# Fused sigmoid attention, Fourier mixing with an MLP and a gated convolution on one core: another way to turn float64 weights into float32, and one more feed-forward group by seven products

## Chip, cores, metric

One core of one Trainium2 chip runs the whole program. Its engines are TensorE (PE; weight loads are PEld), VectorE (DVE), ScalarE (ACT), GpSimd (POOL) and SyncE (SP, which issues the transfers). The metric is device time in microseconds (us), the median of several executions. The reports below come from one further execution, taken by the hardware profiler.

## What is computed

```python
def reference(q, k, v, moe, moe2):                 # q, k, v: 4 x 12 x 448 x 64, float32
    a = sigmoid(q @ k.T / sqrt(64) - log(448)) @ v          # per batch and head
    x = a.transpose(0, 2, 1, 3).reshape(4, 448, 768)
    u = x + real(fft(fft(x, axis=1), axis=2))
    un = (u - mean(u)) / sqrt(var(u) + 1e-6)                # over the last axis
    x = u + maximum(un @ w_ch1, 0) @ w_ch2                  # 768 -> 3072 -> 768
    gate = sigmoid(causal_conv(x, conv_w))                  # 5 taps along the sequence
    return (gate * (x @ w_val)) @ w_out                     # 768 -> 768 -> 768
```

The four weight matrices arrive as float64, drawn from a normal distribution.

## The kernel before

Everything is written by one planner. Jobs are Python generators that yield "my next instruction belongs to this engine and needs these tiles"; the planner (class `Board`, with the estimated durations of class `Clock`) keeps an estimated time per engine and places the waiting jobs' instructions by rank and time, so the order on every engine is fixed when the kernel is built. All instructions are recorded at the helper line L219, so the rows below are told apart by their tiles. An engine runs its list in order: what stands behind a waiting instruction waits too.

The stages, by time in the profiled execution:

- 0 to 182 us: attention. A step is 8 matmuls `ps_s<-q,k`, one ACT sigmoid `sg<-ps_s` and 8 matmuls `ps_m<-sg,v`; there are 84 steps. The Fourier transform (`cd`, `cs`, `k,e`) of each batch, its row means (`ones,tt`) and its variance's factor (`tt,ones`) are placed in between. The first weight blocks are converted here.
- 182 to 800 us: the feed-forward part, in NG = 6 groups of 512 hidden columns. `up` of a group is done in one of two forms. The regular form (`up`, for the groups below REG) does the four batches one by one: 288 matmuls of 128x448 per group, with hi and lo halves of float16 (hi x hi, hi x lo, lo x hi). The form with seven products (`quad`, for the other groups) takes batches in pairs and, by sums of halves of activations (`tb`) and of weights (`w1hi`, `w1lo`), does 4 quads of 63 matmuls, 252 per group, and joins the results on DVE (`c`, `w1lo`, `h`), ACT (`c`, `h`) and POOL (`h<-c,h`). `down` is the same for all groups: 288 matmuls `ps_m<-h,w`, added by DVE into `acc`.
- The sums `tb` are made on POOL by `sums`: a first half once batch 3 is normalised, a second half per pair once `up` of the last regular group has passed that pair.
- 800 us to the end: gates, values (`xs,wv`) and output (`gh,wo`) of the four batches.

Weights: `convert` (L447) fetches a float64 piece of 128x384 (tile `w`), and makes a float32 out of its two 32-bit halves. ACT takes the absolute value of the upper half (`wabs<-w`), DVE clamps it and takes the maximum of each row in the same instruction (`wabs,mx<-wabs`, with a read of the accumulator behind it), DVE shifts (`wabs<-wabs`, or `wf<-wabs` for the first blocks), and two DVE instructions with two inputs bring in the low bits and the sign (`wabs<-w,wabs`). The float32 pieces are spilled to DRAM and read back for scaling and splitting. `peak` (L411) turns a block's row maxima into one maximum: DVE puts them on a diagonal (`pd`), PE multiplies it by ones, DVE reduces and works out the scale (`factors`). PE executes 24 such matmuls in the program. There are 120 pieces: 8 for each block of w_ch1 or w_ch2 (w1[g], w2[g]; 16 per group), and 12 each for w_val and w_out. The blocks w1[0], w2[0] and w1[1], the first 24 pieces, go straight into `wf` without a spill; the others are spilled. A fetched tile has three buffers, and the next fetch of SP waits until the piece that held the buffer is done.

Of the kernel before, what the change touches and what calls it, by code (L numbers as in the profile page):

```python
# [59 lines left out]
DRAM = bass.MemoryType.DRAM  # L60
FIRST = 7
TABLE = 8
ABS_BY = "ACT", "DVE"
W_RANK = 3.5
LEAST = 2.0 ** (896 // 8 - 127)


class Clock:
# [91 lines left out]
    def note(self, e, op, a, k):  # L160
        if op == "matmul":
            out, w, x = a
            n = x.free_size()
            full = x.partition_size() > 64 or w.free_size() > 64
            passes = 1 if x.dtype != F32 else 4 if full else 1
            cost = passes * (max(n / 2400, 0.045) + (0.0018 if passes == 1 else 0.006))
            mode = full, out.partition_size() > 64 or not full
            if mode != self.mode:
                cost += 0.2
                self.mode = mode  # L170
            return self.put("PE", cost, (w, x), (out,), 0.12, tag="mm")
# [170 lines left out]
def body(tc, qd, kd, vd, w1d, w2d, cwd, wvd, wod, cdd, k12d, csd, eyed, out):  # L342
# [68 lines left out]
    def peak(m, nm):  # L411
        yield on("DVE", m, eye)
        t = col(nm + "t")
        V.tensor_reduce(out=t, in_=m, axis=AX.X, op=ALU.max)
        d = keep.tile([128, 128], F32R, tag="pd", bufs=2, name="pd")
        V.tensor_scalar(out=d, in0=eye, scalar1=t, scalar2=None, op0=ALU.mult)
        yield on("PE", d, go=banks(1))
        p = ps_m()
# [4 lines left out]
        done_m(p)
        return g

    def pow2(g, nm, upper=False, e=None):

        e = col(nm + "e") if e is None else e
        if upper:
            V.tensor_scalar(out=e.bitcast(I32), in0=g.bitcast(I32), scalar1=0x07F00000, scalar2=3, op0=ALU.bitwise_and, op1=ALU.logical_shift_left)  # L430
            V.scalar_tensor_tensor(out=e.bitcast(I32), in0=g.bitcast(I32), scalar=0x40000000, in1=e.bitcast(I32), op0=ALU.bitwise_and, op1=ALU.bitwise_or)
        else:
            V.tensor_scalar(out=e.bitcast(I32), in0=g.bitcast(I32), scalar1=0x7F800000, scalar2=None, op0=ALU.bitwise_and)
# [10 lines left out]

    W1N = NT * FG

    def convert(rank, src, m, dst=None, to=None, step=COLS, done=None, hold=None):  # L447

        num = len(src)
        got, ready, gone = [], [], [0] if done is None else done  # L450

        def fetch():
            for k in range(num):
                yield on("SP", go=lambda: gone[0] > k - 3)
                w = ws.tile([128, step], I64, tag="w64", bufs=3, name="w64")
# [17 lines left out]
        board.add(rank, absolute())  # L473
        for k in range(num):
            yield when(lambda: len(ready) > k and (hold is None or hold(k)))
            z, wa = got[k], ready[k]
            lo, hi, f = z[:, :, 0], z[:, :, 1], wa if dst is None else dst[k]
            yield on("DVE", wa)
            if m is None:
                V.tensor_scalar(out=wa, in0=wa, scalar1=LEAST, scalar2=None, op0=ALU.max)  # L480
            else:
                V.tensor_scalar(out=wa, in0=wa, scalar1=LEAST, scalar2=None, op0=ALU.max, op1=ALU.max, accum_out=m[k])
            yield on("DVE", wa)
            V.tensor_scalar(out=f.bitcast(I32), in0=wa.bitcast(I32), scalar1=0x07FFFFFF, scalar2=3, op0=ALU.bitwise_and, op1=ALU.logical_shift_left)
            yield on("DVE", z)
            V.scalar_tensor_tensor(out=f.bitcast(I32), in0=lo, scalar=29, in1=f.bitcast(I32), op0=ALU.logical_shift_right, op1=ALU.bitwise_or)
            yield on("DVE", z)
            V.scalar_tensor_tensor(out=f.bitcast(I32), in0=hi, scalar=-0x40000000, in1=f.bitcast(I32), op0=ALU.bitwise_and, op1=ALU.bitwise_or)
# [1107 lines left out]
```

## Time and profile before

| | |
|---|---|
| median of 3 executions | 1026.77 us (1026.36 to 1028.44) |
| the profiled execution | 1025.13 us |
| its span, first to last instruction | 1023.3 us |
| PE, DVE, ACT, POOL busy | 98%, 77%, 46%, 28% |
| matmuls | 6048 |
| mean granted TensorE clock | 0.996 |

The page gives for every engine the busy time over the span. Matmuls are pipelined and their ends are modelled, so a busy PE is read together with the count of matmuls per stretch. "idle before <-releaser" is time in which an engine stood still ahead of an instruction, and what ended it.

### The profile page before, as it was taken

How to read it: one execution, taken by the hardware profiler on the slowest of the kernel's cores; microseconds unless marked ns; L12 is line 12 of the kernel's file. 1: busy time of each engine (PE TensorE's matmuls, PEld its weight loads, DVE VectorE, ACT ScalarE, POOL GpSimd, SP SyncE). 2: the span in 40 equal slices, each digit the busy share in tenths (PEclk: the TensorE clock that was granted, in tenths of full speed). 3: DMA queues.
4: the chain of work that ended last, by engine and by line, in shares of the span. 5: the costliest groups of instructions: out<-in, count | busy, mean ns of one | idle time of the engine just before them, and what ended most of it. 6: DMA issues, size and time to landing. Idle time of an engine off the chain costs nothing.

```text
span 1023.3 us, 15801 instructions
## 1 busy us (share of the span) xinstructions
PE 1006.0 (98%) x6048; PEld 524.2 (51%) x6048; DVE 791.1 (77%) x1480; ACT 471.4 (46%) x666; POOL 285.8 (28%) x209
## 2 busy tenths in 40 slices
PE   9899899999999999999999999999999999999998
PEld 4344454675555555555555555545555555555554
DVE  4776788888998778968979998989894487767630
ACT  6786767235341354143515451445144687344321
POOL 0103323232768520035503320332033573000000
PEclk9999999999999999999999999999999999999999
DMA  7653240001222366545345435643450120000001
GB/s 232 220 184 99 82 134 11 15 16 47 67 82 70 116 200 224 160 157 187 107 155 183 134 117 176 196 126 114 155 157 30 47 93 1 10 37 37 37 30 70
DMA packets 54547, 110.30 MB, mean 108 GB/s; under 512 B 6456, under 2 KB 30408, under 8 KB 54472
## 3 DMA queue, kind: packets, MB, share of 16 engines
q1 hardware_dynamic: 54472, 109.30, 33.5%
q8 instruction: 47, 0.77, 0.3%
q14 instruction: 28, 0.23, 0.1%
HBM read 84.76 MB, written 24.38 MB: 107 GB/s over the span
## 4 chain that ended last, share of the span: by engine, by line
PE 86%; DVE 8%; issue 2%; ACT 2%; DMA 1%; SPq 0%; DVEq 0%; ACTq 0%
PE ps_m L219 62%; PE ps_s L219 25%; DVE wabs L219 2%; DVE wf L219 1%; DVE tt L219 1%; DVE c L219 1%; DVE acc L219 1%; DVE pm L219 0%; DMA v<-vd 0%; DMA q<-qd 0%; ACT sg L219 0%; ACT h L219 0%; SPq L219 0%; ACT c L219 0%; DVE pd L219 0%
## 5 line engine op out<-in xcount | busy, mean ns | idle before, releaser
L219 PE MATMUL ps_m<-h,w 128*128 128x448 f16 x1728 | 328.8, 353 | 0.0
L219 PEld LDWEIGHTS <-w 128*128 128x128 f16 x2016 | 196.8, 98 | 183.4 <-issue 2.9
L219 PE MATMUL ps_s<-un,w1hi 128*128 128x448 f16 x528 | 143.0, 353 | 0.0
L219 ACT ACTIVATE wabs<-w 128x384 f32<-128x384 f32 x120 | 65.2, 551 | 168.1 <-DMA w<-w2d 44.9
L219 DVE SCALAR_TENSOR_TENSOR wabs<-w,wabs 128x384 int32<-128x384 int32 x192 | 135.9, 708 | 4.7
L219 PEld LDWEIGHTS <-w1hi 128*128 128x128 f16 x888 | 86.3, 98 | 80.0
L219 DVE SCALAR_TENSOR_TENSOR acc<-ps_m,rg,acc 128x448 f32<-128x448 f32 x144 | 97.9, 680 | 35.8 <-PE ps_m L219 32.3
L219 POOL TENSOR_TENSOR w<-wf,w 128x768 f16<-128x768 f32 x24 | 41.1, 1724 | 213.2 <-ACT w L219 213.0
L219 ACT ACTIVATE sg<-ps_s,logb 128x896 f32<-128x896 f32 x84 | 83.9, 1007 | 30.7 <-PE ps_s L219 29.7
L219 PE MATMUL ps_s<-un,w1lo 128*128 128x448 f16 x264 | 93.0, 352 | 0.0
L219 PE MATMUL ps_m<-sg,v 64*64 64x448 f32 x672 | 82.8, 550 | 3.1 <-DVE acc L219 2.1
L219 PE MATMUL ps_s<-q,k 64*64 64x448 f32 x672 | 80.9, 538 | 4.4 <-ACT sg L219 4.4
L219 PE MATMUL ps_m<-xs,wv 128*128 128x448 f16 x432 | 84.6, 353 | 0.0
L219 PE MATMUL ps_m<-gh,wo 128*128 128x448 f16 x288 | 80.8, 352 | 0.0
L219 DVE SCALAR_TENSOR_TENSOR gp<-acc,cw,gp 128x448 f32<-128x448 f32 x84 | 60.3, 718 | 21.9 <-ACT gp L219 19.9
L219 POOL TENSOR_TENSOR h<-c,h 128x896 f16<-128x896 f32 x24 | 46.4, 1934 | 90.2 <-ACT h L219 69.4
L219 DVE TENSOR_SCALAR_CACHE_REDUCE wabs<-wabs 128x384 f32<-128x384 f32 x120 | 65.3, 544 | 2.2 <-ACT wabs L219 2.1
L219 PEld LDWEIGHTS <-w1lo 128*128 128x128 f16 x444 | 43.4, 98 | 40.6
L219 PEld LDWEIGHTS <-wo 128*128 128x128 f16 x432 | 42.3, 98 | 39.5
L219 PEld LDWEIGHTS <-wv 128*128 128x128 f16 x432 | 42.1, 98 | 39.1
L219 ACT ACTIVATE h<-ps_s 128x896 f16<-128x896 f32 x24 | 22.0, 916 | 79.5 <-PE ps_s L219 79.3
L219 PE MATMUL ps_s<-un,w 128*128 128x448 f16 x288 | 57.9, 360 | 0.0
(172 smaller groups left out, 1446.7 us busy)
## 6 DMA issues: line engine op xcount, KB each, us to landing
w<-w1d SPq DMA_DIRECT2D x48, 384.0 KB
w<-w2d SPq DMA_DIRECT2D x48, 384.0 KB
w<-wabs SPq DMA_DIRECT2D x72, 192.0 KB
wf<-w SPq DMA_DIRECT2D x36, 384.0 KB
q<-qd SPq DMA_DIRECT2D x24, 224.0 KB
out<-o SPq DMA_DIRECT2D x24, 224.0 KB
k<-kd SPq DMA_DIRECT2D x23, 224.0 KB
w<-wvd SPq DMA_DIRECT2D x12, 384.0 KB
```

The source lines that it names most:

```text
L219: return f(*a, **k)
```

## The change

1. REG goes from 3 to 2: group 2 is done with seven products too. The second half of `sums` starts when `up` of group 1, not 2, has passed a pair.
2. `convert` works in place in the fetched tile. ACT (or, for the first 24 pieces, ACT or DVE, whichever the planner finds free) makes two passes: the upper half times 2^-112 as float32, and the top byte of the lower half as an integer of three bits. DVE joins the two with two instructions of two inputs. The piece is spilled, and then its magnitudes are summed along the rows by an ACT pass with an accumulator (`w,mx<-f`); for w_val, and where DVE is chosen, DVE takes the exact row maximum with a reduction. The scale exponents are set anew for sums in place of maxima.
3. In `peak`, the matmul with `pd` may be placed on PE only 2.5 us after DVE's estimated time, from PE's 200th us on.
4. `Clock` gives every single-pass matmul 0.0029 instead of 0.0018 us on top of its columns.
5. `pow2` loses the two-instruction form for float64 exponents.

```diff
-UN_EXP = 4
+UN_EXP = -2
...
-REG = 3
+REG = 2
-NABS = 3
+PD = 2.5
...
-ABS_BY = "ACT", "DVE"
+EARLY_BY = "ACT", "DVE"
+LATE_BY = "ACT"
+WBUF = 3
+FBUF = 3
...
-            cost = passes * (max(n / 2400, 0.045) + (0.0018 if passes == 1 else 0.006))
+            cost = passes * (max(n / 2400, 0.045) + (0.0029 if passes == 1 else 0.006))
...
-        yield on("PE", d, go=banks(1))
+        late = ck.at["DVE"] + (PD if ck.at["PE"] > 200 else 0.0)
+        yield on("PE", d, go=lambda: banks(1)() and board.by(late))
...
-                yield when(lambda: len(got) > k and gone[0] > k - NABS)
-                wa = ws.tile([128, step], F32, tag="wabs", bufs=NABS, name="wabs")
-                e = yield on(by, got[k], cost=0.55)
+                yield when(lambda: len(got) > k)
+                w = got[k].bitcast(F32).rearrange("p (n t) -> p n t", t=2)
+                e = yield on(by, w[:, :, 1], cost=0.55)
                 if e == "ACT":
-                    A.activation(out=wa, in_=got[k][:, :, 1].bitcast(F32), func=AF.Abs)
+                    A.activation(out=w[:, :, 1], in_=w[:, :, 1], func=AF.Copy, scale=2.0 ** -112)
                 else:
-                    V.tensor_scalar(out=wa.bitcast(I32), in0=got[k][:, :, 1], scalar1=0x7FFFFFFF, scalar2=None, op0=ALU.bitwise_and)
-                ready.append(wa)
+                    V.tensor_scalar(out=w[:, :, 1], in0=w[:, :, 1], scalar1=2.0 ** -112, scalar2=None, op0=ALU.mult)
+                lo = w.bitcast(I32)[:, :, 0]
+                e = yield on(by, w[:, :, 0], cost=0.55)
+                if e == "ACT":
+                    top = got[k].bitcast(U8).rearrange("p (n t) -> p n t", t=8)[:, :, 3]
+                    A.activation(out=lo, in_=top, func=AF.Copy, scale=2.0 ** -5, bias=-0.484375)
+                else:
+                    V.tensor_scalar(out=lo, in0=lo, scalar1=29, scalar2=None, op0=ALU.logical_shift_right)
+                ready.append(w.bitcast(I32))
+        def join():
...
+                yield when(lambda: len(ready) > k and gone[0] > k - FBUF and (hold is None or hold(k)))
+                lo, hi = ready[k][:, :, 0], ready[k][:, :, 1]
...
+                yield on("DVE", hi, lo)
+                V.scalar_tensor_tensor(out=lo, in0=hi, scalar=-0x80000000, in1=lo, op0=ALU.bitwise_and, op1=ALU.bitwise_or)
+                yield on("DVE", lo, f)
+                V.scalar_tensor_tensor(out=f.bitcast(I32), in0=hi, scalar=3, in1=lo, op0=ALU.logical_shift_left, op1=ALU.bitwise_or)
...
-                V.tensor_scalar(out=wa, in0=wa, scalar1=LEAST, scalar2=None, op0=ALU.max, op1=ALU.max, accum_out=m[k])
-            yield on("DVE", wa)
-            V.tensor_scalar(out=f.bitcast(I32), in0=wa.bitcast(I32), scalar1=0x07FFFFFF, scalar2=3, op0=ALU.bitwise_and, op1=ALU.logical_shift_left)
...
+            if m is not None:
+                e = yield on("DVE" if exact(k) else by, f, cost=0.75)
+                if e == "ACT":
+                    A.activation(out=ready[k].bitcast(F32)[:, :, 1], in_=f, func=AF.Abs, accum_out=m[k])
+                else:
+                    V.tensor_reduce(out=m[k], in_=f, axis=AX.X, op=ALU.max, apply_absolute_value=True)
             gone[0] += 1
```

The program as a whole has 36 matmuls of 128x448 fewer, since one group's `up` goes from 288 to 252. On ACT, 119 passes `wabs<-w` give way to 224 passes `w<-w` and 89 with an accumulator; on DVE, 120 clamps with an accumulator and 120 shifts are gone, 240 joins remain, and 31 reductions and 16 passes come in.

**ACT, in the quads of a late group.** `w_...` are fetched float64 pieces, `f_...` their float32. Before:

```order
L219 ACTIVATE w1lo<-ps_m 128x448
L219 ACTIVATE c<-c 128x896
L219 ACTIVATE h<-c 128x896
L219 ACTIVATE wabs<-w_6310 128x384
L219 ACTIVATE wabs<-w_6345 128x384
L219 ACTIVATE c<-c 128x896
L219 ACTIVATE h<-c 128x896
L219 ACTIVATE w1lo<-ps_m 128x448
L219 ACTIVATE wabs<-w_6386 128x384
L219 ACTIVATE wabs<-w_6452 128x384
L219 ACTIVATE c<-c 128x896
L219 ACTIVATE h<-c 128x896
```

After, in a like place:

```order
L222 ACTIVATE c<-c 128x896
L222 ACTIVATE h<-c 128x896
L222 ACTIVATE w_6520<-w_6520 128x384 x2
L222 ACTIVATE w_6438,mx<-f_6538 128x384
L222 ACTIVATE c<-c 128x896
L222 ACTIVATE h<-c 128x896
L222 ACTIVATE w_6550<-w_6550 128x384 x2
L222 ACTIVATE w1lo<-ps_m 128x448
L222 ACTIVATE w_6520,mx<-f_6568 128x384
L222 ACTIVATE w_6581<-w_6581 128x384 x2
L222 ACTIVATE w_6550,mx<-f_6610 128x384
L222 ACTIVATE c<-c 128x896
```

A piece now has three instructions on ACT, and the last of them, with `mx`, stands behind the first two of the next piece.

**DVE, around the first maximum of w_val** (`wvt` is the row maxima's maximum, `pd` the diagonal, `wvg` the reduction of PE's product). Before:

```order
L219 SCALAR_TENSOR_TENSOR wabs<-w_6386,wabs 128x384
L219 TENSOR_TENSOR c<-ps_s,w1lo 128x896
L219 TENSOR_TENSOR c<-ps_s,c 128x448
L219 SCALAR_TENSOR_TENSOR wabs<-w_6386,wabs 128x384
L219 TENSOR_REDUCE wvt<-mx 128x1
L219 TENSOR_SCALAR pd<-eye,wvt 128x128
L219 TENSOR_SCALAR wabs,mx<-wabs 128x384
L219 TENSOR_SCALAR wabs<-wabs 128x384
L219 SCALAR_TENSOR_TENSOR wabs<-w_6452,wabs 128x384
L219 TENSOR_TENSOR c<-ps_s,c 128x896
L219 SCALAR_TENSOR_TENSOR wabs<-w_6452,wabs 128x384
L219 TENSOR_REDUCE wvg<-ps_m 128x1
```

After:

```order
L222 SCALAR_TENSOR_TENSOR acc_104<-ps_m,rg,acc_104 128x448
L222 SCALAR_TENSOR_TENSOR w_6156<-w_6156 128x384
L222 SCALAR_TENSOR_TENSOR f_6208<-w_6156 128x384
L222 TENSOR_REDUCE mx<-f_6208 128x1
L222 TENSOR_REDUCE wvt<-mx 128x1
L222 TENSOR_SCALAR pd<-eye,wvt 128x128
L222 TENSOR_TENSOR c<-ps_m,w1lo 128x448
L222 SCALAR_TENSOR_TENSOR w_6188<-w_6188 128x384
L222 TENSOR_TENSOR w1lo<-ps_m,w1lo 128x448
L222 SCALAR_TENSOR_TENSOR f_6254<-w_6188 128x384
L222 TENSOR_REDUCE wvg<-ps_m 128x1
L222 TENSOR_SCALAR factors<-wvg 128x1
```

A piece has two joins and a reduction where it had four instructions; between `pd` and `wvg` four instructions stand where there were five.

**PE, at the row sums of squares of the last batch** (`ones,tt`) and at the matmuls that spread its factor (`tt,ones`). Before, the sums:

```order
L219 LDWEIGHTS w_770
L219 MATMUL ps_s<-un,w_770 128x448
L219 MATMUL ps_m<-ones,tt 112x1 x24
L219 LDWEIGHTS w_770
L219 MATMUL ps_s<-un,w_770 128x448
```

and the factor, 30 matmuls later:

```order
L219 LDWEIGHTS w_770
L219 MATMUL ps_s<-un,w_770 128x448
L219 MATMUL ps_m<-tt,ones 128x112 x4
L219 LDWEIGHTS w_770
L219 MATMUL ps_s<-un,w_770 128x448
```

After, the second and larger part of the sums (a first part of x8 stands 6 matmuls ahead of it):

```order
L222 LDWEIGHTS w_788
L222 MATMUL ps_s<-un,w_788 128x448
L222 MATMUL ps_m<-ones,tt 112x1 x16
L222 LDWEIGHTS w_788
L222 MATMUL ps_s<-un,w_788 128x448
```

and the factor, 18 matmuls `un,w` and 6 `h,w` later:

```order
L222 LDWEIGHTS w_2431
L222 MATMUL ps_m<-h,w_2431 128x448
L222 MATMUL ps_m<-tt,ones 128x112 x4
L222 LDWEIGHTS w_2431
L222 MATMUL ps_m<-h,w_2431 128x448
```

The sums are split, and the first matmuls `h,w` of `down` of group 0 have moved ahead of the factor; before, they came 102 matmuls behind it. At the first `h,w`, PE has 216 matmuls `un,w` behind it; at the factor of before it had 186.

## Rows read from the trace of the kernel before

**Rows 1.** The page's first part, PE's share: busy us, share, instructions.

```profile
PE 1006.0 (98%) x6048; PEld 524.2 (51%) x6048; DVE 791.1 (77%) x1480; ACT 471.4 (46%) x666; POOL 285.8 (28%) x209
```

**Rows 2.** Chain that ended last: start us, us, what.

```profile
252.16 19.31 PE ps_s L219 x102
...
381.45 54.68 PE ps_m L219 x290
```

**Rows 3.** Stretches of 20 us: busy us and count by engine, PE clock, DMA.

```profile
500.00:520.00 20.00, 20.00 (x108) 10.36 (x106) 19.86 (x27) 4.87 (x7) 9.31 (x6) 1.00 0.04 15
...
680.00:700.00 20.00, 18.74 (x100) 9.59 (x99) 19.04 (x41) 8.71 (x12) 4.72 (x3) 1.00 0.49 147
```

**Rows 4.** PE in order of time: matmuls of `pd` after 200 us that waited.

```profile
293.63 0.33 PE L219 MATMUL ps_m<-pd,ones_r 128*128 128x128 f32 x1 [0.61 <-DVE pd L219]
...
489.85 0.33 PE L219 MATMUL ps_m<-pd,ones_r 128*128 128x128 f32 x1 [0.30 <-DVE pd L219]
...
655.70 0.33 PE L219 MATMUL ps_m<-pd,ones_r 128*128 128x128 f32 x1 [0.44 <-DVE pd L219]
...
686.25 0.30 PE L219 MATMUL ps_m<-pd,ones_r 128*128 128x128 f32 x1 [1.26 <-DVE pd L219]
...
855.96 0.33 PE L219 MATMUL ps_m<-pd,ones_r 128*128 128x128 f32 x1 [0.48 <-DVE pd L219]
```

**Rows 5.** PE in order of time, the three longest waits of attention.

```profile
34.98 0.33 PE L219 MATMUL ps_m<-pd,ones_r 128*128 128x128 f32 x1 [1.19 <-DVE pd L219]
...
47.96 0.98 PE L219 MATMUL ps_s<-q,k 64*64 64x448 f32 x8 [2.72 <-ACT sg L219]
...
178.00 3.72 PE L219 MATMUL ps_m<-sg,v 64*64 64x448 f32 x24 [2.10 <-DVE acc L219]
```

**Rows 6.** PE in order of time, around the last batch's row sums.

```profile
238.41 4.79 PE L219 MATMUL ps_m<-ones,tt 128*112 128x1 f32 x48
...
251.02 1.15 PE L219 MATMUL ps_m<-tt,ones 112*128 112x112 f32 x8 [0.45 <-DVE tt L219]
```

**Rows 7.** Stretches of 2 us behind these sums, columns as in rows 3.

```profile
244.00:246.00 2.00, 2.00 (x7) 0.87 (x6) 1.49 (x1) 1.97 (x3) 2.00 (x2) 0.50 0.03 8
246.00:248.00 2.00, 2.00 (x9) 0.84 (x8) 2.00 (x1) 1.85 (x3) 2.00 (x3) 0.66 0.00 0
```

**Rows 8.** POOL in order of time: the four low halves of w2[0].

```profile
244.45 6.44 POOL L219 TENSOR_TENSOR w<-wf,w 128x768 f16<-128x768 f32 x4
```

**Rows 9.** Groups by form, conversion: busy us, mean ns, idle before.

```profile
L219 DVE TENSOR_SCALAR_CACHE_REDUCE wabs<-wabs 128x384 f32<-128x384 f32 x120 | 65.3, 544 | 2.2 <-ACT wabs L219 2.1
...
L219 ACT ACTIVATE wabs<-w 128x384 f32<-128x384 f32 x119 | 65.0, 553 | 168.1 <-DMA w<-w2d 44.9 <-DMA w<-w1d 35.9 <-DMA w<-wod 29.1
...
L219 DVE TENSOR_SCALAR wabs<-wabs 128x384 int32<-128x384 int32 x96 | 47.3, 493 | 2.7
...
L219 ACT ACTIVATION_READ_ACCUMULATOR xs<-acc 128x1 f32 x8 | 1.5, 187 | 0.0
```

**Rows 10.** Longer stretches, columns as in rows 3: attention; one late group.

```profile
0.00:180.00 180.00, 169.74 (x1580) 81.86 (x1584) 135.51 (x278) 128.50 (x163) 40.87 (x38) 1.00 0.43 138
...
551.00:652.00 101.00, 100.99 (x535) 52.25 (x534) 94.72 (x179) 42.18 (x60) 20.70 (x12) 1.00 0.49 155
```

**Rows 11.** DVE and POOL in order of time, end of attention.

```profile
174.25 1.99 DVE L219 TENSOR_SCALAR wf<-wabs 128x384 int32<-128x384 int32 x1
...
174.12 1.90 POOL L219 TENSOR_TENSOR un<-tt,un 128x896 f16<-128x896 f32 x1 [6.30 <-ACT un L219]
```

**Rows 12.** POOL in order of time: second half of `tb`, first pair.

```profile
443.85 2.04 POOL L219 TENSOR_TENSOR tmp<-un 128x448 f32<-128x448 f16 x2
...
478.56 1.04 POOL L219 TENSOR_TENSOR un<-tmp,un 128x448 f16<-128x448 f32 x1 [1.95 <-ACT un L219]
```

**Rows 13.** Groups by form, joining of the quads, as in rows 9.

```profile
L219 ACT ACTIVATE c<-c 128x896 f32<-128x896 f32 x24 | 22.8, 950 | 59.9 <-DVE c L219 59.9
...
L219 DVE TENSOR_TENSOR c<-ps_s,w1lo 128x896 f32<-128x896 f32 x12 | 13.0, 1087 | 6.9 <-PE ps_s L219 6.9
```

More of the change, by code (lines that the diff above doesn't have):

```diff
@@ L13 @@
 I64 = mybir.dt.int64
+U8 = mybir.dt.uint8
 AF = mybir.ActivationFunctionType
@@ L32 @@
 X_EXP = 3
-W1_EXP = 1
-W2_EXP = 9
-UN_EXP = 4
+W1_EXP = 7
+W2_EXP = 14
+UN_EXP = -2
 X2_EXP = 14
 WV_EXP = 1
-WO_EXP = 9
+WO_EXP = 14
 G_EXP = -10
@@ L424, in peak, with pow2 @@
         return g
-    def pow2(g, nm, upper=False, e=None):
+    def pow2(g, nm, e=None):
         e = col(nm + "e") if e is None else e
[L429 to L433, printed above, removed]
+        V.tensor_scalar(out=e.bitcast(I32), in0=g.bitcast(I32), scalar1=0x7F800000, scalar2=None, op0=ALU.bitwise_and)
         V.tensor_scalar(out=e, in0=e, scalar1=2.0 ** -90, scalar2=2.0 ** 90, op0=ALU.max, op1=ALU.min)
@@ L445, in body, with convert @@
     W1N = NT * FG
-    def convert(rank, src, m, dst=None, to=None, step=COLS, done=None, hold=None):
+    def convert(rank, src, m, dst=None, to=None, step=COLS, done=None, hold=None, exact=lambda k: False):
         num = len(src)
@@ L453, in fetch @@
             for k in range(num):
-                yield on("SP", go=lambda: gone[0] > k - 3)
-                w = ws.tile([128, step], I64, tag="w64", bufs=3, name="w64")
+                yield on("SP", go=lambda: gone[0] > k - WBUF)
+                w = ws.tile([128, step], I64, tag="w64", bufs=WBUF, name="w64")
                 Q.dma_start(out=w, in_=src[k])
-                got.append(w.bitcast(I32).rearrange("p (n t) -> p n t", t=2))
-        by = ABS_BY if rank < 4 else "ACT"
-        def absolute():
+                got.append(w)
@@ L462, in absolute, with parts @@
+        by = EARLY_BY if rank < 4 else LATE_BY
+        def parts():
             for k in range(num):
[L463 to L465 removed]
+                yield when(lambda: len(got) > k)
+                w = got[k].bitcast(F32).rearrange("p (n t) -> p n t", t=2)
+                e = yield on(by, w[:, :, 1], cost=0.55)
                 if e == "ACT":
[L467 removed]
+                    A.activation(out=w[:, :, 1], in_=w[:, :, 1], func=AF.Copy, scale=2.0 ** -112)
@@ new lines, in parts @@
+                ready.append(w.bitcast(I32))
+        def join():
+            for k in range(num):
+                yield when(lambda: len(ready) > k and gone[0] > k - FBUF and (hold is None or hold(k)))
+                lo, hi = ready[k][:, :, 0], ready[k][:, :, 1]
+                f = ws.tile([128, step], F32, tag="f32", bufs=FBUF, name="f32") if dst is None else dst[k]
+                yield on("DVE", hi, lo)
+                V.scalar_tensor_tensor(out=lo, in0=hi, scalar=-0x80000000, in1=lo, op0=ALU.bitwise_and, op1=ALU.bitwise_or)
+                yield on("DVE", lo, f)
+                V.scalar_tensor_tensor(out=f.bitcast(I32), in0=hi, scalar=3, in1=lo, op0=ALU.logical_shift_left, op1=ALU.bitwise_or)
+                joined.append(f)
@@ L472, in convert @@
+        joined = []
         board.add(rank, fetch())
-        board.add(rank, absolute())
+        board.add(rank, parts())
+        board.add(rank, join())
         for k in range(num):
-            yield when(lambda: len(ready) > k and (hold is None or hold(k)))
-            z, wa = got[k], ready[k]
-            lo, hi, f = z[:, :, 0], z[:, :, 1], wa if dst is None else dst[k]
-            yield on("DVE", wa)
-            if m is None:
-                V.tensor_scalar(out=wa, in0=wa, scalar1=LEAST, scalar2=None, op0=ALU.max)
-            else:
-                V.tensor_scalar(out=wa, in0=wa, scalar1=LEAST, scalar2=None, op0=ALU.max, op1=ALU.max, accum_out=m[k])
-            yield on("DVE", wa)
-            V.tensor_scalar(out=f.bitcast(I32), in0=wa.bitcast(I32), scalar1=0x07FFFFFF, scalar2=3, op0=ALU.bitwise_and, op1=ALU.logical_shift_left)
[L485 to L488, printed above, removed]
@@ L489, in convert @@
+            yield when(lambda: len(joined) > k)
+            f = joined[k]
             if to is not None:
@@ L545, in stream @@
         board.add(4, scaling())
-        yield from convert(4, src, ms, None, to, done=done, hold=lambda k: all(e[2] in kept for e in ends[:max(0, sum(x[0] <= k for x in ends) - 1)]))
+        yield from convert(4, src, ms, None, to, done=done, exact=lambda k: next(e[2][0] for e in ends if k < e[0]) == "wv", hold=lambda k: all(e[2] in kept for e in ends[:max(0, sum(x[0] <= k for x in ends) - 1)]))
     def again(key):
```

3 lines of the change are left out of this document (1 added, 2 removed).

## The prediction

> **What bounds the kernel now.** The first view is the page's share of busy time: PE is busy for 98% of the span [rows 1]. Since matmuls are pipelined, that share alone says little, so the second view is the chain that ended last, where long pieces are PE alone: 102 matmuls in 19.31 us and 290 in 54.68 us, 0.189 us each [rows 2]. The third is PE's count in stretches of 20 us: a full one holds 108 matmuls of 128x448, 0.185 us each, even where DVE is busy for 19.86 of 20 us; one with a wait holds 100 [rows 3]. So behind attention the end is set by PE's number of matmuls plus the places where PE stands still, and whatever the other engines gain is worth something only at such a place.
>
> These places are, read from PE in order of time: five matmuls of `pd` after 200 us that waited for DVE, 0.61 + 0.30 + 0.44 + 1.26 + 0.48 = 3.1 us [rows 4]; some waits in attention, the three longest 1.19, 2.72 and 2.10 us [rows 5]; the matmul of the last batch's factor, 0.45 us [rows 6]; and a fall of the clock right behind 48 one-column matmuls that took 4.79 us [rows 6]. The granted clock is 0.50 in the next stretch of 2 us, which is the lower level of 1.2 GHz, and 0.66 in the one behind it [rows 7]. In these 4 us PE made 16 matmuls where 108 per 20 us are 21.6, so the fall cost about 5.6 x 0.189 = 1.1 us at least, and with its edges some 1.7 us (half of the 2 + 0.68/0.5 = 3.4 us at 0.50).
>
> **The matmuls of group 2.** 288 regular ones become 252, at 0.189 us each [rows 2]: 36 x 0.189 = **-6.8 us**. All of them lie on PE in a stretch where nothing else sets the end [rows 3]. The Trainium skill ("Perfetto Trace Analysis", section "Identifying the Most-Contended Engine") says that matmul busy time doesn't show how close TensorE is to its limit, and asks for the weight loads' busy share instead. That share is 51% here [rows 1]; by this rule PE might have room left and the 36 matmuls be worth nothing, and the sum would be 6.8 us less. The counts per stretch [rows 3] speak against it, and I take them.
>
> **The matmuls with `pd` placed later.** Each waits for a short DVE chain that the planner had estimated too early. With 2.5 us of room against waits of 0.30 to 1.26 us [rows 4], all five should be gone: -3.1 us, and I take **-3.0 us**; the bounds are 0, where DVE is late by more than that, and -3.1. What waits behind is the scale on DVE and then the scaling of a block on ACT and POOL, up to 2.5 us later; weight blocks are needed tens of us later, except for w2[0], below.
>
> **The last batch's variance.** The one-column matmuls are split in two runs, x8 and x16 where x24 stood, and `down` of group 0 stands in front of the factor's matmul. The wait of 0.45 us is covered by it, and the fall of the clock, which came after one unbroken run, should be less or gone: 0 to -2.2 us, I take **-2.0 us**. The price of the cover: PE now needs w2[0] at its first `h,w`. POOL finished its low halves at 244.45 + 6.44 = 250.9 us [rows 8]. PE's first `h,w` stands behind 216 matmuls `un,w` where the factor, at 251.0 us, stood behind 186: 251.0 + 30 x 0.189 = 256.7 us, less the 2.2 us above and what attention gains, so 253 to 255 us. The slack is 2 to 4 us; a wait here would take back up to 3 us, with nothing behind it on PE to fill in.
>
> **The conversion.** DVE loses 120 clamps of 0.544 us with their accumulator reads and 120 shifts of about 0.49 us [rows 9], and gets 47 instructions of the same size: some 65 + 59 - 26 = 98 us less, and it waits for ACT's passes instead. ACT loses 119 passes of 0.553 us and gets 224 of them and 89 with an accumulator. No row shows a pass over every eighth byte or one that writes in place; the nearest is the pass over every second word, 0.553 us, and I take that (bounds 0.5 and 1.1 us, twice it). For the accumulating ones I add the 0.187 us of the read [rows 9]: 0.74 us. ACT's net is 105 x 0.553 + 89 x 0.74 = +124 us. A late group has 16 pieces: ACT goes from 42.18 us in a stretch of 101 us to 42.2 + 16 x (0.553 + 0.74) = 63 us, DVE from 94.72 to about 94.7 - 16 x 1.1 = 77 us [rows 10]. Both stay below PE, so behind 200 us this edit is worth **0 us** by itself; PE's 108 per 20 us covers it. If ACT's `c`, `h` come late because a pass ahead of them waits for a transfer or a join, up to +5 us come out.
>
> In attention it is another matter, since PE waits there for `sg` of ACT and `acc` of DVE [rows 5], and ACT is busy for 128.5 of 180 us [rows 10]. By the order, ACT has there 17 passes and 3 accumulations where 13 absolute values stood, +4 x 0.553 + 3 x 0.74 = +4.4 us, and three 128x896 instructions `un` go behind the stage: about the same load, in another order. The wait of 2.10 us came after a shift on DVE that took 1.99 us [rows 11] instead of about 0.49 [rows 9], beside a POOL instruction of 1.90 us that began 0.13 us earlier [rows 11]. Shifts of that kind are mostly gone. The Trainium skill ("SBUF", section "Who interferes with whom") has it that `tensor_scalar` and GpSimd lock each other out of a shared port pair for a whole instruction; the trace agrees with 1.99 us. The same section says that a DVE instruction with two SBUF inputs contends with GpSimd's reads as well, and the joins are such. By the first rule alone the stage would gain 2.1 us, by both it would keep part. I take **-1 us** for the stage: the three waits of rows 5 sum to 6.0 us, any may go and others come. The bounds are -6 and, with ACT's passes at 1.1 us, 17 x 0.55 = +9.
>
> **Group 2 by seven products.** DVE gets five joins per quad of at most 1.087 us, ACT two instructions `c` and two `h` of about 0.95 us [rows 13]: at most 22 and 15 us in a group, from which the regular form's eight `h` on each engine go. Against 77 and 63 us of about 102 this fits. The sums `tb`: the first pair's second half took from 443.85 to 479.6 us on POOL [rows 12], 36 us. It now starts when group 1's `up` passes the pair, about 354 us (half of that `up`'s 288 x 0.189 = 54 us ahead of 381.45 [rows 2]) and, for the second pair, 381 us, so it ends at about 390 and 417 us; the quads of group 2 start when `down` 1 ends, 381.45 + 54.68 = 436 us [rows 2], less what was gained, and the second pair's 24 us later. Slack 40 us: **0 us**.
>
> **The sum.** -6.8 - 3.0 - 2.0 - 1.0 = -12.8 us. The profiled execution was 1025.13 us with a span of 1023.3; the median is 1026.77, 1.6 us above it. 1025.1 - 12.8 = 1012.3, and in terms of the median **1014.0 us**.
>
> **The rivals.**
> *Only the columns, or only the waits.* The waits for DVE turn up at other matmuls of `pd`, or at w2[0], and the 6.8 us remain: about 1026.8 - 6.8 = 1020 us. The rule on weight loads is the same case from the other side: the 36 matmuls give nothing and the waits go, 1026.8 - 6.0 = 1020.8 us. For it: all waits are DVE's, by an estimate of the planner that may be off elsewhere. Against: DVE gets lighter by some 98 us.
> *Attention gets smooth.* The waits of rows 5 go, 6 us in place of 1: 1009 us, or less with smaller ones. For it: DVE's slow shifts go. Against: one of the three waits is ACT's, which gets no lighter there.
> *A piece's round trip (slower).* A fetched tile is now held through two ACT passes, two joins, and the ACT pass with `mx`, which stands behind the next piece's passes and behind `c` and `h`. With three buffers and 16 pieces per 102 us, a round trip of 3 x 102/16 = 19 us is the point from which PE waits for weights. Each us beyond is 16/3 = 5.3 us per group, over four groups 21 us; one us over gives 1014 + 21 = 1035 us. For it: ACT waited 44.9 us for transfers of w2 alone already [rows 9]. Against: it had 168 us idle there, and PE lost nothing.
> *Attention worse.* ACT's passes at twice the price: +9 in place of -1 in the stage, 1014 + 10 = 1024 us, and a little more where the same passes hold up `c` and `h` later: about 1025 to 1028 us, within 0.2%.
>
> **Chances.** Forecast (1010 to 1018 us) 0.60; smooth attention (1004 to 1010) 0.12; only columns or only waits (1018 to 1023) 0.13; attention worse (1025 to 1028) 0.06; round trip 0.09. A measurement of this kernel can tell a difference of about 0.2%, 2 us, from none: faster than 1024.7 us 0.85, within 0.06, slower 0.09. A range of 1006 to 1024 us leaves out the last two and the lower part of smooth attention, under 0.2.
>
> **What would show it.** 6012 matmuls, and full stretches of 108 per 20 us from 260 to 800 us. No `pd` matmul after 200 us with an idle time for DVE. The granted clock near 1.0 between 240 and 250 us, and no wait for w2[0] at the first `h,w`. ACT's passes near 0.55 us, the accumulations near 0.74, ACT at about 59% and DVE near 68%. The forecast is wrong if PE's stretches hold fewer than 108 while ACT is behind with `c` or `sg`, if `tb` or a weight block ends a wait of PE, or if attention ends later than 182 us by more than a few us.

## The result, and the profile after

| | before | after |
|---|---|---|
| median | 1027.43 us (1026.36 to 1028.44, 4 runs) | 1012.05 us (1009.61 to 1014.13, 4 runs) |
| profiled execution, its span | 1025.13, 1023.3 us | 1009.61, 1007.8 us |
| ratio, 95% interval | | 0.985 (0.9824 to 0.9875) |

The change makes the kernel 15.4 us faster; 12.8 had been forecast, in another composition, as the experiments show. The page's first part, to be read against [rows 1]:

```profile
PE 996.7 (99%) x6012; PEld 520.1 (52%) x6012; DVE 701.6 (70%) x1172; ACT 573.1 (57%) x965; POOL 293.3 (29%) x212
```

36 matmuls are gone, DVE lost 90 us and ACT gained 102. Two stretches of 20 us that answer to [rows 3], then attention's and a late group's, which answer to [rows 10] (columns as in [rows 3]):

```profile
500.00:520.00 20.00, 20.00 (x109) 10.38 (x106) 14.08 (x27) 5.73 (x13) 0.00 (x0) 1.00 0.52 168
680.00:700.00 20.00, 20.00 (x109) 10.41 (x107) 15.95 (x30) 17.03 (x33) 3.79 (x2) 1.00 0.55 166
...
0.00:180.00 180.00, 172.40 (x1594) 82.41 (x1595) 137.00 (x264) 132.65 (x176) 36.67 (x36) 0.99 0.43 138
538.00:639.00 101.00, 101.00 (x537) 52.45 (x536) 77.85 (x130) 63.01 (x122) 22.45 (x13) 1.00 0.53 165
```

The two stretches of 20 us hold 109 matmuls each, and from 260 to 900 us every stretch of 20 us holds 107 to 109; there is no longer one that holds 100. In a late group DVE went from 94.72 to 77.85 us of 101 and ACT from 42.18 to 63.01; the prediction had 77 and 63. The waits of PE (who waited for whom: us in all, times, longest):

```profile
PE ps_m L222 <- DVE zl L222: 3.3, 1, 3.3
PE ps_s L222 <- ACT sg L222: 1.7, 2, 1.3
PE ps_m L222 <- DVE acc L222: 1.1, 1, 1.1
PE ps_m L222 <- DVE logb L222: 1.1, 1, 1.1
PE ps_m L222 <- DVE tt L222: 0.2, 1, 0.2
```

The five waits of [rows 4] for `pd` are gone, and all that is left lies ahead of 180 us. The longest is at the end of attention, where before had 2.10 us [rows 5]. PE, DVE and POOL there, in order of time, and the stretch of 2 us behind it:

```profile
174.82 3.69 PE L222 MATMUL ps_m<-sg,v 64*64 64x448 f32 x24 [3.29 <-DVE zl L222]
...
171.92 2.32 DVE L222 TENSOR_SCALAR w<-w 128x384 f32<-128x384 f32 x2
174.16 1.13 DVE L222 SCALAR_TENSOR_TENSOR zl<-ps_m,rt,zh 113x385 fp32r<-113x385 f32 x2
...
172.13 1.89 POOL L222 TENSOR_TENSOR un<-tt,un 128x896 f16<-128x896 f32 x1 [3.08 <-ACT un L222]
...
176.00:178.00 2.00, 2.00 (x16) 0.54 (x8) 1.28 (x2) 0.00 (x0) 0.00 (x0) 0.50 0.04 8
```

DVE's two passes `w<-w` take 2.32 us, since a POOL instruction runs from 172.13 to 174.02; `zl` stands behind them, and PE's last matmuls of attention behind `zl`. Then the clock is at 0.50, the level of 1.2 GHz. The kernel before has such a fall behind its 2.10 us as well, which the prediction did not count:

```profile
178.00:180.00 2.00, 2.00 (x17) 0.79 (x21) 2.00 (x3) 0.00 (x0) 1.97 (x2) 0.78 0.67 184
180.00:182.00 2.00, 2.00 (x13) 0.53 (x6) 0.12 (x1) 0.23 (x1) 1.11 (x1) 0.50 0.06 20
```

With 0.87 in the next stretch that is 0.22 x 2 + 0.50 x 2 + 0.13 x 2 = 1.7 us lost before; after, 0.50 and then 0.66 lose 1.7 us too. Around the last batch's variance, which answers to [rows 6] and [rows 7]:

```profile
244.67 3.32 PE L222 MATMUL ps_m<-ones,tt 128*112 128x1 f32 x32
...
252.82 1.30 PE L222 MATMUL ps_m<-h,w 128*128 128x448 f16 x6
253.95 1.04 PE L222 MATMUL ps_m<-tt,ones 112*128 112x112 f32 x8
...
246.00:248.00 2.00, 2.00 (x21) 1.96 (x21) 1.90 (x5) 0.00 (x0) 0.00 (x0) 0.91 0.70 186
248.00:250.00 2.00, 2.00 (x6) 0.76 (x5) 1.93 (x6) 0.10 (x1) 1.32 (x1) 0.50 0.76 226
250.00:252.00 2.00, 2.00 (x9) 0.94 (x8) 1.04 (x5) 1.48 (x5) 0.00 (x0) 0.74 0.40 152
```

The factor's matmuls `tt,ones` have no wait in front of them now, and the first `h,w` at 252.82 us none either. But the clock falls as before: 0.91, 0.50 and 0.74 in three stretches of 2 us are 0.09 x 2 + 0.50 x 2 + 0.26 x 2 = 1.7 us lost, where [rows 7] gave 1.7 as well. The conversion on ACT, by form (busy us, mean ns, idle before):

```profile
L222 ACT ACTIVATE w<-w 128x384 int32<-128x384 uint8 x113 | 61.9, 548 | 0.0
L222 ACT ACTIVATE w<-w 128x384 f32<-128x384 f32 x111 | 61.2, 551 | 41.7 <-DMA w<-w1d 13.2 <-DMA w<-wvd 12.7 <-DMA w<-w2d 9.8
L222 ACT ACTIVATE w<-f 128x384 f32<-128x384 f32 x84 | 46.4, 553 | 73.9 <-DVE f L222 73.8
...
L222 ACT ACTIVATION_READ_ACCUMULATOR w<-f 128x1 f32 x84 | 15.4, 184 | 0.0
```

The pass over every eighth byte costs 0.548 us, as much as one over words (0.551), and the pass with an accumulator 0.553 + 0.184 = 0.74 us: the values that the prediction took. ACT waited 73.8 us for the joins ahead of its sums, and PE noticed none of it.

### The profile page after: what moved, and what is told of

Its sections match the earlier page's. It is cut to its first block, busy times and chain, and to the rows that moved or that the text cites. A ratio compares the mean times of both kernels' runs of the same rounds, so it can differ in the third digit from the quotient of the medians.

```text
span 1007.8 us, 15709 instructions
## 1 busy us (share of the span) xinstructions
PE 996.7 (99%) x6012; PEld 520.1 (52%) x6012; DVE 701.6 (70%) x1172; ACT 573.1 (57%) x965; POOL 293.3 (29%) x212
## 4 chain that ended last, share of the span: by engine, by line
PE 93%; DVE 4%; ACT 2%; DMA 1%; issue 0%; ACTq 0%; SPq 0%; DVEq 0%
PE ps_m L222 67%; PE ps_s L222 26%; ACT sg L222 1%; DVE pm L222 1%; DVE w L222 1%; DVE tt L222 1%; DVE wf L222 1%; DVE acc L222 0%; DVE un L222 0%; DMA v<-vd 0%; DVE vm L222 0%; DMA w<-w1d 0%; ACT w L222 0%; DVE wm L222 0%; ACT acc L222 0%
## 5 line engine op out<-in xcount | busy, mean ns | idle before, releaser
L222 ACT ACTIVATE w<-w 128x384 f32<-128x384 f32 (+2 forms) x226 | 113.4, 546 | 41.7 <-DMA w<-w1d 13.2
L222 PEld LDWEIGHTS <-w1hi 128*128 128x128 f16 x864 | 83.9, 98 | 77.8
L222 PE MATMUL ps_s<-un,w1hi 128*128 128x448 f16 x384 | 104.0, 353 | 0.0
L222 DVE SCALAR_TENSOR_TENSOR w<-w 128x384 int32<-128x384 int32 (+1 forms) x121 | 84.9, 702 | 15.7 <-ACT w L222 15.5
L222 POOL TENSOR_TENSOR h<-c,h 128x896 f16<-128x896 f32 x32 | 62.1, 1942 | 112.5 <-ACT h L222 104.5
L222 ACT ACTIVATE w<-f 128x384 f32<-128x384 f32 x84 | 46.4, 553 | 73.9 <-DVE f L222 73.8
L222 DVE SCALAR_TENSOR_TENSOR f<-w 128x384 int32<-128x384 int32 x96 | 71.3, 743 | 2.1
L222 PE MATMUL ps_s<-un,w1lo 128*128 128x448 f16 x192 | 67.7, 352 | 0.0
L222 ACT ACTIVATE c<-c 128x896 f32<-128x896 f32 x32 | 30.3, 948 | 55.4 <-DVE c L222 55.4
```

The source lines that it names most:

```text
L222: return f(*a, **k)
```

## The experiments

**Which part brings how much.** Seven combinations were timed against the kernel before, whose median in those sessions was 1025.6 to 1027.4 us. First, group 2 taken back in the changed kernel:

```diff
-REG = 2
+REG = 3
```

> The changed kernel with REG back at 3, so group 2 is regular again: 36 matmuls of 128x448 more. Theory (PE's columns are the bound in that group): 36 x 0.189 = 6.8 us more than the changed kernel, 1012.05 + 6.8 = 1018.9 us, no new wait of PE between 260 and 800 us. Rival (the 36 matmuls lie beside another engine's work, by the weight loads' share of 52% PE has room): 1012 us, and the gain of 15 us lies elsewhere.

Measured: 1018.6 us (1017.65 to 1018.97, 6 runs). The group by seven products is worth 6.6 us in the changed kernel, where 36 x 0.189 = 6.8 had been worked out. The rival, by which PE had room, falls.

Group 2 alone, in the kernel before:

```diff
-REG = 3
+REG = 2
```

> The kernel before with REG 2 alone: group 2 by seven products, conversion as before. Theory (DVE has room for it even without the new conversion): 1027.43 - 6.8 = 1020.6 us, with the waits at pd as before. Rival (the lighter DVE is what makes the third regular group dispensable: DVE is busy for about 88 of 110 us in the stretch of group 2 and gets some 13 to 15 us more on 102): DVE falls behind with the joins and PE waits for c or w1lo, 1027 us or more.

Measured: 1030.7 us (1028.61 to 1036.85, 12 runs), ratio 1.0039 (1.002 to 1.0059): slower, although 36 matmuls are gone. PE's waits in its profile:

```profile
PE ps_m L219 <- DVE pd L219: 8.2, 8, 2.7
PE ps_s L219 <- ACT sg L219: 6.5, 4, 3.2
PE ps_m L219 <- POOL w L219: 2.4, 3, 1.2
PE ps_m L219 <- ACT w L219: 1.2, 1, 1.2
```

The waits for `pd` went from 4.8 us in before to 8.2, and near 390 us PE waited four times, 3.6 us in all, for the halves of w2[1]. On DVE the reduction of PE's product for that block came 10 us behind PE's matmul, since two pieces' conversion and two `h`, the second waiting for ACT, stood ahead of it. Waits are about half of the loss. All of PE's waits together went from 13.8 us to 22.5, and what the falls of the clock lose, summed over the stretches of 2 us as above, from 3.4 us in two places to 11.9 in five. These 8.7 and 8.5 us, less 6.8 for the matmuls, are 10.4 of the 11.4 us that the two spans differ by (1034.7 and 1023.3). This profiled execution, at 1036.85 us, was the slowest of its twelve, so the split need not be that of the median.

The place of `pd` taken back in the changed kernel:

```diff
-PD = 2.5
+PD = 0.0
```

> The changed kernel with PD = 0, so the matmuls of pd stand where the planner's estimate puts them. Theory (the estimate is too early by the length of DVE's small instructions, whatever DVE's load): waits of PE for pd come back, as in the kernel before 3 to 4 us in sum, 1015.5 us. Rival (a DVE with 90 us less work is on time by itself): no waits, 1012 us.

Measured: 1013.7 us (1013.53 to 1016.01, 5 runs), 1.6 us more than with it. One wait came back, not five:

```profile
677.28 0.33 PE L222 MATMUL ps_m<-pd,ones_r 128*128 128x128 f32 x1 [1.07 <-DVE pd L222]
```

So neither side is wholly right: a lighter DVE is on time for most of them by itself. The intervals of this ratio (0.9844 to 0.99) and of the change's (0.9824 to 0.9875) overlap, so the size of 1.6 us is not shown.

The place of `pd` alone, in the kernel before:

```diff
+PD = 2.5
...
-        yield on("PE", d, go=banks(1))
+        late = ck.at["DVE"] + (PD if ck.at["PE"] > 200 else 0.0)
+        yield on("PE", d, go=lambda: banks(1)() and board.by(late))
```

> The kernel before with only the 2.5 us for pd. Theory: the five waits after 200 us go, 3.1 us as idle time and 3.8 with their edges: 1027.43 - 3.8 = 1023.6 us. Rival (DVE is too loaded, it is late by more than the room, or the waits turn up elsewhere): 1026 to 1028 us.

Measured: 1024.1 us (1021.5 to 1030.97, 12 runs), ratio 0.9977 (0.9953 to 1.0002). No `pd` waited behind 200 us in its profile, as the theory had it; the interval just reaches one. In the tail a new wait stands instead, for `xs`, the scaled activations, whose scale hangs on a later `pd` as well:

```profile
PE ps_m L220 <- DVE xs L220: 2.8, 1, 2.8
...
PE ps_m L220 <- DVE pd L220: 1.7, 2, 1.2
```

The conversion alone (the changed kernel with REG 3, PD 0 and the old 0.0018 in the clock):

> The new conversion alone: REG 3, PD 0, the old 0.0018 in the clock. Theory (conversion takes work off DVE, so the scale chains and the acc joins come sooner; the end moves by the waits of PE that this removes): after_reg3 has 1018.6 and PD was worth 1.6 in the changed kernel, so about 1020 to 1022 us, 5 to 7 less than before. Rival (conversion is worth nothing by itself since PE covers it, as the prediction had it): 1026 to 1027 us.

Measured: 1017.5 us (1016.41 to 1018.14, 6 runs), ratio 0.9894 (0.9866 to 0.9922): 9.7 us less than before, more than either side had. In its profile attention ends with a wait of 1.59 us for `acc`, and the waits for `pd` are down to 1.8 us in four:

```profile
PE ps_m L222 <- DVE acc L222: 2.0, 2, 1.6
PE ps_m L222 <- DVE pd L222: 1.8, 4, 0.7
PE ps_s L222 <- ACT sg L222: 1.7, 2, 1.3
...
173.70 2.49 PE L222 MATMUL ps_m<-sg,v 64*64 64x448 f32 x24 [1.59 <-DVE acc L222]
```

Its last matmuls of attention end at 173.70 + 2.49 = 176.2 us where they ended at 178.00 + 3.72 = 181.7 in before [rows 5], so 5.5 us of the 8.1 that the two spans differ by (1023.3 and 1015.2) are attention's; of the rest, 1.9 us are waits for `pd` behind 200 us, 3.1 us in before and 1.2 here, and some 0.7 us are not assigned. In all, PE's waits went from 13.8 us to 7.5, those for DVE from 9.4 to 4.9. The clock gives nothing in sum: the fall at the end of attention is not there, and the one at the last batch's variance costs 3.4 us in place of 1.7.

The old conversion with both other parts (REG 2 and the 2.5 us, in the kernel before):

> The kernel before with REG 2 and the 2.5 us for pd, conversion as before. With REG 2 alone PE waited 8.2 us for pd and 3.6 us for w2[1] (POOL w and ACT w), and the time was 1030.7. Theory (DVE's load is the cause, by two ways, pd too early and the scale's chain queued behind conversion on DVE): the waits for pd behind 200 us go, the one for w2[1] stays or grows by up to 2.5 us, 1022 to 1026 us, over the 1020.6 that the 36 matmuls alone would give. Rival (pd's place was the whole trouble): 1018 us or less, that is 1024.1 less 6.8.

Measured: 1017.6 us (1013.22 to 1019.67, 6 runs), ratio 0.9907 (0.9879 to 0.9935). The rival was right: with `pd` placed later, the old conversion carries group 2 too. PE's waits for `pd` and for the weights in its profile:

```profile
PE ps_m L220 <- DVE pd L220: 1.7, 2, 1.2
PE ps_m L220 <- DVE w1lo L220: 1.3, 1, 1.3
```

The 1.7 us for `pd` lie in attention, and the waits for w2[1] are gone, because in this order that block's maximum comes 9 us sooner on DVE (356.8 us instead of 365.8). That this came with the place of `pd` is seen; why the planner then put the block earlier was not followed up.

| conversion | REG | `pd` | median, us |
|---|---|---|---|
| old | 3 | as estimated | 1025.6 to 1027.4 |
| old | 3 | later | 1024.1 |
| old | 2 | as estimated | 1030.7 |
| old | 2 | later | 1017.6 |
| new (old clock) | 3 | as estimated | 1017.5 |
| new | 3 | later | 1018.6 |
| new | 2 | as estimated | 1013.7 |
| new | 2 | later | 1012.05 |

(The last three rows have 0.0029 in the clock, the others 0.0018.) The parts don't add: the conversion gives 9.7 us alone and 5.6 on top of the other two (5.0 with the old clock, by the 1012.6 us below); the place of `pd` gives 3.1 alone, 13.1 with group 2 and nothing with the new conversion at REG 3, where the clock's term changed along with it; group 2 costs 3.5 alone and gives 6.5 where `pd` is placed later, with either conversion. Every edit also makes the planner write a new order, so each of these differences holds the edit's own worth and that of the new order; the runs don't separate the two.

**The planner's clock.**

```diff
-            cost = passes * (max(n / 2400, 0.045) + (0.0029 if passes == 1 else 0.006))
+            cost = passes * (max(n / 2400, 0.045) + (0.0018 if passes == 1 else 0.006))
```

> The changed kernel with the old cost of a matmul in the planner's clock (0.0018 for 0.0029). Theory (only the order's estimate moves, by 0.0011 us a matmul, which adds up to some 5 us over the program, and the waits that the 2.5 us cover): 1011 to 1014 us. Rival (with it the planner believes PE ahead, and pd, tb and c are placed too early): waits of PE behind 400 us, 1015 us or more.

Measured: 1012.6 us (1010.01 to 1015.15, 6 runs), the same. Attention ends earlier in this order, and the tail gives it back: PE waits for `xs` at 943.64 us, and the clock falls behind it.

```profile
943.64 2.03 PE L222 MATMUL ps_m<-xs,wv 128*128 128x448 f16 x5 [2.76 <-DVE xs L222]
...
944.00:946.00 2.00, 2.00 (x7) 0.85 (x6) 0.30 (x1) 0.00 (x0) 0.00 (x0) 0.50 0.03 8
```

The same with the 2.5 us for the weights' `pd` only:

```diff
-        late = ck.at["DVE"] + (PD if ck.at["PE"] > 200 else 0.0)
+        late = ck.at["DVE"] + (PD if ck.at["PE"] > 200 and nm != "x2" else 0.0)
```

> The changed kernel with 0.0018 in the planner's clock and the 2.5 us only for the weights' pd, not for the one of the activations (x2). With 0.0018 alone PE waits 2.8 us for xs near 942 us, and the clock is at 0.5 after it. Theory (the later pd of x2 is what made xs late): that wait and that fall go, 2.8 + 1.7 = 4.5 us less than the 1012.6 of that run, 1008 us. Rival (xs is late for another reason): wait as before, 1012 to 1013 us.

Measured: 1009.9 us (1008.92 to 1011.17, 6 runs), ratio 0.9836 (0.981 to 0.9863). The wait and the fall are gone, here in the stretch that held them, and of 4.5 us expected 2.7 came out:

```profile
940.00:950.00 10.00, 10.00 (x55) 5.16 (x54) 5.56 (x9) 3.53 (x6) 0.00 (x0) 1.00 0.13 48
```

One matmul with `pd` in the tail waited instead (0.77 us more than its usual step, at 841 us). It is the fastest of the kernels here by its median; its interval overlaps the changed kernel's.

**The wait at the end of attention.** The first try takes DVE out of the passes for all of the first 24 pieces:

```diff
-EARLY_BY = "ACT", "DVE"
+EARLY_BY = "ACT"
```

> The changed kernel with the first 24 pieces' passes on ACT only, so DVE makes no pass there. At the end of attention PE waits 3.3 us for zl on DVE, which stands behind two such passes that took 2.3 us beside a POOL instruction, and the clock is at 0.50 after it. Theory: both go, 3.3 + 1.7 = 5 us less, 1007 us. Rival (ACT has no room in attention, and sg comes later): 1012 us or more, with waits of PE for ACT sg.

Measured: 1027.3 us (1023.5 to 1028.99, 12 runs), as slow as before. The wait for `zl` is gone. The rival's sign is there, but small: PE waits 5.0 us for `sg` in seven waits, where it was 1.7 in two. Most of the loss lies behind attention, where the order changed:

```profile
PE ps_m L222 <- POOL tt L222: 9.5, 1, 9.5
PE ps_s L222 <- ACT sg L222: 5.0, 7, 1.5
PE ps_m L222 <- DVE tt L222: 4.9, 2, 4.1
```

Between 190 and 206 us PE waits 4.1 us for DVE's `tt` and, two matmuls later, 9.5 us for POOL's, ahead of a batch's row sums and with nothing else placed in between; the granted clock is 0.50 from 196 to 210 us. So this run doesn't tell what the passes alone are worth.

The second gives DVE's float pass the form with an accumulator:

```diff
-                    V.tensor_scalar(out=w[:, :, 1], in0=w[:, :, 1], scalar1=2.0 ** -112, scalar2=None, op0=ALU.mult)
+                    V.tensor_scalar(out=w[:, :, 1], in0=w[:, :, 1], scalar1=2.0 ** -112, scalar2=None, op0=ALU.mult, op1=ALU.max, accum_out=keep.tile([128, 1], F32, tag="junk", bufs=2, name="junk"))
```

> The changed kernel with DVE's float passes of the first 24 pieces in the form that also writes an accumulator (to a column that nobody reads). Theory (a tensor_scalar without accumulator and POOL lock each other out for a whole instruction, and the form with an accumulator doesn't): no such pass takes over 0.7 us, and the wait at the end of attention falls from 3.3 us to under 2, 1009 to 1011 us. Rival (any DVE instruction beside a POOL one is slow, or the wait is a matter of order): the wait stays at 3 us, 1012 us.

Measured: 1016.1 us (1011.74 to 1017.55, 6 runs), with the wait for `zl` at 3.3 us. DVE and POOL there:

```profile
175.38 0.54 DVE L222 TENSOR_SCALAR_CACHE_REDUCE w<-w 128x384 f32<-128x384 f32 x1
...
175.85 1.84 DVE L222 TENSOR_SCALAR w<-w 128x384 int32<-128x384 int32 x1
...
175.59 1.89 POOL L222 TENSOR_TENSOR un<-tt,un 128x896 f16<-128x896 f32 x1 [3.08 <-ACT un L222]
```

The pass with the accumulator began before POOL's instruction and took 0.54 us; the next one, without, began inside it and took 1.84. So it doesn't tell the forms apart, only that who starts second pays. The run is slower for another reason: of the 6.4 us by which its span is longer than the changed kernel's (1014.2 and 1007.8), 1.4 are more waits of PE and some 5 the clock, which falls at 128 us too and loses 3.4 us in place of 1.7 at the end of attention and again at the last batch's variance.

The third gives the passes to ACT from the 150th us on, so that joins stand on DVE there:

```diff
-                e = yield on(by, w[:, :, 1], cost=0.55)
+                e = yield on(by if ck.at["PE"] < 150 else LATE_BY, w[:, :, 1], cost=0.55)
...
-                e = yield on(by, w[:, :, 0], cost=0.55)
+                e = yield on(by if ck.at["PE"] < 150 else LATE_BY, w[:, :, 0], cost=0.55)
```

> The changed kernel with the two passes on ACT from PE's 150th us on, so before that everything stays as it is. DVE then has two joins of about 0.6 to 0.7 us at the end of attention where two passes took 2.3 us beside a POOL instruction of 1.9 us. Theory (the pass without accumulator is locked out by POOL for most of an instruction, a join is only slowed): PE's wait for zl falls from 3.3 us to about 2.2 to 2.5, 1011 us; the fall of the clock behind it stays, since PE still waits for over 2 us. Rival (joins are locked out as long): 3.3 us or more, 1012 us.

Measured: 1011.7 us (1010.19 to 1014.26, 6 runs), with a wait of 3.7 us. A join is locked out for as long as a pass was:

```profile
174.34 0.55 DVE L222 SCALAR_TENSOR_TENSOR w<-w 128x384 int32<-128x384 int32 x1
174.92 2.12 DVE L222 SCALAR_TENSOR_TENSOR wf<-w 128x384 int32<-128x384 int32 x1
...
174.54 4.25 POOL L222 TENSOR_TENSOR un<-tt,un 128x896 f16<-128x896 f32 x2 [3.08 <-ACT un L222]
```

The fourth takes POOL's instruction away instead:

```diff
-LOW_BY = "DVE", "POOL"
+LOW_BY = ("DVE",)
```

> The changed kernel with the low halves of un (un<-tt,un) on DVE alone, so POOL has none of its 1.9 us instructions at the end of attention; DVE has the same instructions there in nearly the same order (two passes, then zl). Theory (a DVE instruction that starts while such a POOL instruction runs waits for it to end, be it a pass or a join): the two passes take about 0.36 us each, 0.7 in place of 2.3, and PE's wait for zl falls from 3.3 us to about 1.7; the fall of the clock behind it is shorter or gone, and 1.6 to 3.3 us come out, 1009 to 1010.5 us, unless the twelve instructions of 1.09 us that DVE gets make it late elsewhere. Rival (the wait is a matter of DVE's order, not of POOL): 3.3 us as before, 1012 us or more.

Measured: 1010.05 us (1008.62 to 1011.31, 4 runs), ratio 0.9855 (0.9833 to 0.9877). DVE has the same two passes there, then `zl`, and POOL nothing:

```profile
171.89 0.62 DVE L222 TENSOR_SCALAR w<-w 128x384 f32<-128x384 f32 x2
172.43 1.14 DVE L222 SCALAR_TENSOR_TENSOR zl<-ps_m,rt,zh 113x385 fp32r<-113x385 f32 x2
...
173.09 2.49 PE L222 MATMUL ps_m<-sg,v 64*64 64x448 f32 x24 [1.59 <-DVE zl L222]
...
174.00:176.00 2.00, 2.00 (x23) 0.67 (x16) 1.65 (x2) 0.56 (x2) 0.00 (x0) 1.00 0.03 8
176.00:178.00 2.00, 2.00 (x14) 1.57 (x13) 1.77 (x3) 1.09 (x3) 1.07 (x1) 1.00 0.00 0
```

The passes take 0.62 us together in place of 2.32, the wait is 1.59 us, near the 1.7 expected, and the clock stays at 1.00 behind it. That settles the cause of 1.7 of the 3.3 us: the POOL instruction, not DVE's order. The other 1.6 us stay. Over the whole kernel the gain is within the spread (the ratio is 0.9855, the change's 0.985). The row sums of the last batch stand in one run of 48 in this order, behind a new wait of 0.9 us for ACT `tt`; they take 7.85 us, and the clock falls further there:

```profile
240.00:250.00 10.00, 9.07 (x53) 7.12 (x51) 4.25 (x5) 9.54 (x13) 6.02 (x4) 0.78 0.02 5
250.00:260.00 10.00, 9.74 (x42) 5.33 (x41) 7.73 (x8) 1.46 (x4) 5.92 (x6) 0.70 0.08 16
```

That is 0.22 x 10 + 0.30 x 10 = 5.2 us lost, where the changed kernel loses 1.7.

## Why the prediction was right, point by point

- **Group 2, -6.8 us.** Right in the changed kernel: 6.6 by the two medians. The Trainium skill's measure ("Perfetto Trace Analysis", section "Identifying the Most-Contended Engine") would have left PE room at a weight loads' share of 52%; the measurement decides against reading it that way here. (The section names the share of the peak rate beside the loads' share; the prediction left that out.)
- **`pd`, -3.0 us.** The waits went, as said, all five. But the term was laid to the wrong part: with the new conversion the place of `pd` is worth 1.6 us by the medians, within the noise, and with REG 3 nothing. Most of the waits go by either edit.
- **Conversion, 0 us behind 200 and -1 in attention.** This is the step that failed. Alone it gives 9.7 us: PE's 108 per 20 us do cover DVE's work, but PE's waits in those very rows are for DVE, and with less work on DVE PE waits for it 4.9 us in all in place of 9.4. The prediction had "all waits are DVE's" as an argument for a rival and didn't draw the conclusion that removing 90 us of DVE's work is a way to remove them. In the whole change the error was small because the waits can go only once; what was under-sized is attention: its end went from 181.7 to 174.82 + 3.69 = 178.5 us, -3.2 in place of -1.
- **The last batch's variance, -2.0 us.** The wait of 0.45 us was covered. The clock's fall was not: 1.7 us before and after, although the longest run of one-column matmuls went from 4.79 to 3.32 us. The term should have been -0.45. What makes the clock fall there stays open: a run of 48 in one lost 1.7 us in before and 5.2 in the last run above.
- **w2[0] at its first use.** No wait; 252.82 us in the place of 253 to 255.
- **Group 2's sums and joins, 0 us.** No wait of PE between 260 and 1000 us.
- **The sum, by the profiled executions.** -6.8 for the matmuls, -3.9 for `pd` with its edges (the steps at those five matmuls were longer than usual by 0.77, 0.46, 0.60, 1.42 and 0.64 us), -3.2 for attention, -0.5 for the variance: -14.4 of the 15.5 that the two spans differ by. Some 1.1 us are spread over steps too small to name. That the forecast came within 2.6 us was in part luck: the variance's term was 1.5 us too large, and attention's 2.2 us and `pd`'s 0.9 us too small.
- **The rivals.** "Only the columns, or only the waits" is out. The round trip of a piece, with 73.8 us of waiting on ACT in it, didn't reach PE. ACT's passes cost the single price. Of the rule on the shared port (the Trainium skill, "SBUF", section "Who interferes with whom") both sentences are borne out: a pass (2.32 us for two) and a join (2.12 us) wait for POOL's instruction, and without it two passes take 0.62 us. At the end of attention it was the first sentence that counted, not the second: the prediction had instructions of that kind as mostly gone, but the change puts 16 `tensor_scalar` passes of the first pieces on DVE, and one of them, begun inside POOL's instruction there, took 2.05 us where the one ahead of it took 0.36.

## What to carry to other kernels

Where one engine is at its rate and stops only for a second one, unloading the second is worth what the stops cost, even if it looks covered on average; price it at the stops, and expect two edits that remove the same stops not to add up. Before saving work on the bounding engine, remove its stops: the same 36 matmuls cost 3.5 us or gave 6.5, by where the matmuls with `pd` stood, and with them the rest of the order. Where a planner writes the order anew for each edit, look at the new order before laying a difference to the edit: one constant that moves a few passes to ACT cost 15 us, most of it by stops of PE elsewhere. A fixed delay that keeps one kind of matmul from waiting too early can make another late, so give it to those that need it.

## What was not expected of the hardware

The spread between executions of one kernel goes with the granted clock: 17 executions of the kernel before in one session went from 1023.45 us at a mean granted clock of 0.998 to 1032.15 at 0.990, and 0.008 x 1025 = 8.2 us is about the difference of 8.7. A stop of PE can cost more than itself: behind the wait of 2.76 us for `xs` came a stretch at 0.50, behind the 3.29 us at the end of attention another, and behind the 1.59 us of the last run none. But the length of the stop doesn't decide it alone. Behind 1.41 us for `acc` at 128 us the clock fell in the run with the accumulator, and behind the same 2.10 us at the end of attention it fell in the kernel before and not in the run with the place of `pd` alone, where the stop ends at 177.10 us:

```profile
170.00:180.00 10.00, 7.90 (x63) 4.13 (x63) 8.81 (x12) 5.68 (x8) 4.77 (x3) 1.00 0.14 41
```

It is at 1.00 in the next 10 us too. So a single profiled execution doesn't show that an edit brought or took away such a fall.
